# Loading all weight tiles of the eighth octet last in a fused linear-attention and spectral-mixing kernel

## The chip, the cores and the metric

The kernel runs on one core of a Trainium2 chip. The metric is the device time of one execution in microseconds (us); the span in a profile, from the first to the last instruction, is some 2 us shorter. A core has five engines that run side by side and wait for each other by semaphores: PE (matrix products, with its weight loads shown as PEld), DVE (elementwise work and reductions), ACT (activations, copies), POOL (elementwise work, and here the issuing of most transfers) and SP (issues transfers). Matrix products go to PSUM, eight banks in all; the other engines bring the results to SBUF. Transfers between the main memory and SBUF run on 16 DMA engines.

## What is computed

Two steps follow each other: a linear attention with a learned feature map, and a spectral mixing layer on its output.

```python
def phi(x):
    proj = np.einsum('bhsd,df->bhsf', x, w_phi)
    proj = proj - np.max(np.abs(proj), axis=-1, keepdims=True)
    return np.concatenate([np.exp(proj), np.exp(-proj)], axis=-1)
q_p, k_p = phi(q), phi(k)
kv = np.einsum('bhsf,bhsd->bhfd', k_p, v)
z = np.sum(k_p, axis=2)
num = np.einsum('bhsf,bhfd->bhsd', q_p, kv)
den = np.einsum('bhsf,bhf->bhs', q_p, z)[..., None] + 1e-06
x = num / den                      # as (batch, seq, heads * head_dim)

X = np.fft.rfft(x, axis=1)         # the first 64 modes are mixed, each by its own matrix
Yr = np.einsum('bmd,mde->bme', Xr, w_r) - np.einsum('bmd,mde->bme', Xi, w_i)
Yi = np.einsum('bmd,mde->bme', Xr, w_i) + np.einsum('bmd,mde->bme', Xi, w_r)
u = x + np.fft.irfft(Y, n=S, axis=1)
out = u + np.maximum(u @ w_ch, 0.0)
```

Batch 8, 8 heads, sequence 576, head size 64 (so 512 channels), 128 features, 64 modes. The matrices `w_r` and `w_i` are 64 x 512 x 512 each, in 4-byte floats, and are by far the most of what has to be read.

## The kernel before

**Tiles.** The 512 channels that go into the mixing are four groups `g` of 128 (two heads each), the 64 modes are eight octets `o` of eight. A weight tile holds, for one group and one octet, the eight matrices of either `w_r` or `w_i`: 64 tiles of 1024 KB each after the cast to 2-byte floats, keyed `(g, w)` with `w = 2 * o + i`. POOL issues their loads (`wload`, L341), most of them into a rotation of nine buffers `wt` (pool `pw`, L84); six tiles of the first group have homes in memory that is still free then, among them halves of `yacc`.

**Attention stage.** A unit is one group and two batches, 16 units in all. The loop from L504 runs over them as a pipeline: while one unit's q is exponentiated, the next one's k is, and so on. Each turn loads k, q and v of a later unit on POOL's queue and ends its part of `x` in `xs`; `freq` and `keep_x` transform a unit's rows to frequencies and put them into `XTb[g % 2]`, so that the rows of group 0 are overwritten by those of group 2, and those of 1 by those of 3. When the fourth unit of a group is done, the keys of the group's tiles are put into `mixq` (L521). `some(n)` (L489) takes keys from it in each turn (eight in the first turn, then three, once four): `mix` (L462) multiplies the frequency rows by the tile, in eight matmuls of 32 rows, and then `next_w(1)` (L360) issues the next load in the order of `wq`. The sum over groups is kept in `yacc` (512 4-byte floats per partition for each octet): group 0 is copied there by ACT, the others added by DVE.

**Order of the tiles** (L352 to L354): all 16 of group 0, all 16 of group 1, twelve of group 2, twelve of group 3 (octets 0 to 5), and then octet 6 of groups 2 and 3 (four tiles) and octet 7 of groups 2 and 3 (four tiles). The two groups of these last octets are summed in one PSUM tile; the sum of groups 0 and 1 is added from `yacc`.

**Loop at the end** (from L922). It takes the tiles that the attention stage has not used. After a mix it calls `next_w(1)`, but for three places (`left not in (19, 9, 8)`), as four of the nine buffers serve other tiles from now on (`yTa`, `zall`, `yall`, `yl`). When the last group of an octet is mixed, the octet's sum `yst` is transposed into `yTa` (octets 0 to 5) or, for octets 6 and 7, also multiplied by `w_ch` (`zst`) and sent by `put` (L818) to `yl`, with four small transfers: on POOL's queue for octet 6, on SP's for octet 7.

Between the mixes `fill(n)` (L813) takes entries from the list `todo`: 36 products (`product`: a chunk of `x` is transposed and multiplied by `w_ch`, the result is kept in `xw`; the first ones carry the tables of the inverse transform, on DVE, along), eight relays (`relay`: the octets so far, of one batch, are transposed into `yall` and multiplied by `w_ch` into `zall`), and 36 absorbs (`Absorb.all`: the modes of the octets so far are transformed back and added to the chunk in `xs` and in `xw`). For 14 of the absorbs (`aside`) the addition to `xw` is done by POOL. The count per mix is worked out from the number of entries left. All of `todo` is done before the last mix.

**After the last mix** comes a fixed order: the octet's sum, its transposes, `zst`, the transform of the last modes for all chunks (`Last`), the rectifier, the sum, and the stores on SP.

All engines' instructions stay in the order in which they are written (`keep_in_program_order`), so the order on each queue is the program's, and a waiting instruction holds up what stands behind it on its engine. POOL's queue holds tile loads, k, q and v loads, the aside additions and octet 6's `yl` transfers.

Of the kernel before, what the change touches and what calls it, by code (L numbers as in the profile page):

```python
# [44 lines left out]
def kernel(  # L45
# [303 lines left out]
        return wt  # L349

    wts = {}
    wq = [(g, mg) for g in range(2) for mg in range(2 * NO)]  # L352
    wq += [(g, mg) for g in (2, 3) for mg in range(12)]
    wq += [(g, 2 * o + i) for o in (6, 7) for g in (2, 3) for i in range(2)]  # L354
    order = list(wq)
    wq.remove((0, 5))
    wq.insert(1, (0, 5))
# [101 lines left out]
                                  op0=ALU.mult, op1=ALU.add)  # L459
    pys = {}  # L460

    def mix(g, w, wt, XT, bank):  # L462

        o, i = w // 2, w % 2
        late = g >= 2 and o >= 6
        first, last = i == 0 and not (late and g == 3), i == 1 and not (late and g == 2)
        if first:
            pys[o] = bank()
        py = pys[o]
        for r in range(2):  # L470
            for j in range(4):
                pe.matmul(
                    py[32 * j:32 * j + 32, :],
                    lhsT=XT[:, i, r, :, :, :, 4 * o + j].rearrange("p t x b -> p (t x b)"),
                    rhs=wt[:, j, r, :], start=(first and r == 0), stop=(last and r == 1),
                )
        if last and g == 0:
            act.copy(yacc[:, o, :], pys.pop(o))
        elif last and g < NG - 1:
            dve.tensor_tensor(  # L480
                out=yacc[:, o, :], in0=pys.pop(o), in1=yacc[:, o, :], op=ALU.add)
# [22 lines left out]
    for n in range(-2, len(units) + 1):  # L504
        P, Q, K, R = (unit(n + i) for i in (-1, 0, 1, 2))
        X = 0 if n < 4 or n == len(units) else 6 if n == 4 else 3
        if Q:
            Q.exp_q(0)
        if K:
            K.rows_k(0)  # L510
            K.exp_k(0)
        if Q:
            Q.weigh_v2()
            if unit(n + 2):
                unit(n + 2).load_v(sp if n + 2 == len(units) - 1 else pool)
        if P:
            P.freq()
            assert not any(key[0] == P.g - 2 for key in mixq)
            P.keep_x()
            if P.bp == NP - 1:  # L520
                mixq += [key for key in order if key[0] == P.g and (P.g < 2 or key[1] < 12)]  # L521
        if Q:
            Q.cols_q(1)
            Q.exp_q(1)
        some(1 if X else 0)
        if K:
            K.rows_k(1)
            K.exp_k(1)
        if Q:
            Q.kv()  # L530
        some(2 if n == 4 else 0)
        if K:
            K.rows_q(0)
            K.rows_k(2)
            K.rows_q(2)
            K.rows_q(1)
        if Q:
            Q.cols_q(2)
            Q.keep_kv()
            Q.exp_q(2)  # L540
        if K:
            K.exp_k(2)
            K.weigh_v()
        some(1 if X else 0)
        if R:
            R.turn_k(0)
        if K:
            K.shift_q()
        if R:
            R.turn_k(1)  # L550
        if Q:
            Q.num(0)
        if K:
            K.cols_q(0)
        if R and unit(n + 4):
            unit(n + 4).load_k()
        if Q:
            Q.num(6)
        if R:
            R.turn_q(0)  # L560
            R.turn_q(1)
            if unit(n + 4):
                unit(n + 4).load_q()
        if Q:
            Q.num(12)
        some(X - 2 + (n == 12) if X else 0)
        if n == -1:
            forward_table()
        if n < 3:
            next_w((2, 3, 2, 3, 2)[n + 2])  # L570
        elif n == 3:
            next_w(1)
        if n == 6:
            pool.dma_start(wchb, moe_w_ch.rearrange("(dc p) e -> p dc e", p=128))
    mixq += order[-8:]
    pm_cm.__exit__(None, None, None)
    pin_cm.__exit__(None, None, None)
    ps1_cm.__exit__(None, None, None)
# [200 lines left out]

    def relay(b):  # L780

        at = slice(0, 6 + (b < 2))
        n = 16 * at.stop
        cols = [yTa[:, dc, b, at].rearrange("p o k -> p (o k)") for dc in range(4)]
        py, pz = two_banks()
        py = py.bitcast(BF16)[:, 0:512]
        for dc in range(4):
            pe.transpose(py[:n, 128 * dc:128 * dc + 128], cols[dc], ident_b)
        for dc in range(4):
            pe.matmul(pz[:n], lhsT=cols[dc], rhs=wchb[:, dc, :],  # L790
                      start=(dc == 0), stop=(dc == 3))
        dve.tensor_copy(yall[:n, b], py[:n])
        act.copy(zall[:n, b], pz[:n])
# [8 lines left out]
        if chunks[i] in stored:  # L802
            ch[i].back_x()

    todo = [ch[0].turn] + [lambda i=i: product(i) for i in range(len(ch))]
    tail = [c.all for c in full]
    for at, b in ((24, 1), (22, 0), (17, 3), (14, 2), (7, 5), (5, 4)):
        tail.insert(at, lambda b=b: relay(b))
    tail = [lambda: relay(6), todo[-2], lambda: relay(7), todo[-1]] + tail
    A = len(tail)  # L810
    todo[-2:] = tail

    def fill(n):  # L813
        for _ in range(n):
            if todo:
                todo.pop(0)()

    def put(src, o, copies):  # L818
        for s in copies:
# [102 lines left out]
    while mixq:  # L922
        key = mixq.pop(0)
        g, o, i = key[0], key[1] // 2, key[1] % 2
        if key not in wts:
            next_w(1)
        if not mixq:
            assert not todo
            for c in seq[:2]:
                c.base(1)  # L930
            for c in (seq[0], seq[2]):
                c.base(0)
        mix(*key, wts.pop(key), XTb[g % 2], bank)
        left = len(mixq)
        if left not in (19, 9, 8):
            next_w(1)
        if left > 8:
            n = -(-max(len(todo) - A - 2, 0) // (left - 8))
        elif left == 8:
            n = 2  # L940
        else:
            n = math.ceil(len(todo) / max(left - 0.6, 0.4)) if left else 0
        if g == NG - 1 and i == 1:
            end = left == 0
            py = pys.pop(o)
            yst = pb.tile([128, DMODEL], BF16, name="yst")
            pt = [bank([128, 2, 128], BF16) for h in range(2)]
            yT = [pb.tile([128, 2, 128], BF16, name=f"yT{h}") if o > 5 else None
                  for h in range(2)]
            for h in range(2):  # L950
                dve.tensor_tensor(out=yst[:, H * h:H * h + H], in0=py[:, H * h:H * h + H],
                                  in1=yacc[:, o, H * h:H * h + H], op=ALU.add)
            if o > 5:
                put(yst, o, (0, 2))
            if not end:
                fill(min(n, 1))
            for h in range(2):
                for dc in range(2):
                    pe.transpose(pt[h][:, dc, :],
                                 yst[:, H * h + 128 * dc:H * h + 128 * dc + 128], ident_b)  # L960
                src = pt[h].rearrange("p c (k b) -> p c b k", b=B_)
                into = yTa[:, 2 * h:2 * h + 2, :, o] if o < 6 else None
                if h:
                    dve.tensor_copy(*((into, src) if o < 6 else (yT[h], pt[h])))
                else:
                    act.copy(*((into, src) if o < 6 else (yT[h], pt[h])))
            if o < 6:
                fill(n - 1)
                continue
            if o == 6:  # L970
                for h in range(2):
                    dve.tensor_copy(
                        yTa[:, 2 * h:2 * h + 2, 0:2, 6],
                        yT[h].rearrange("p c (k b) -> p c b k", b=B_)[:, :, 0:2])
            if end:
                seq[0].straight(0)
                seq[0].keep_p()
                seq[2].straight(0, (0,))
            else:
                fill(1)  # L980
            cut = (slice(0, 384), slice(384, DMODEL))
            pz = [bank([128, e.stop - e.start]) for e in cut]
            for e in range(2):
                for h in range(2):
                    for dc in range(2):
                        pe.matmul(
                            pz[e], lhsT=yT[h][:, dc, :], rhs=wchb[:, 2 * h + dc, cut[e]],
                            start=(h == dc == 0), stop=(h == dc == 1))
            zst = pb.tile([128, DMODEL], BF16, name="zst")
            act.copy(zst[:, cut[0]], pz[0])  # L990
            dve.tensor_copy(zst[:, cut[1]], pz[1])
            put(zst, o, (1, 3))
            fill(n - 2)
        else:
            fill(n)
    assert not todo
# [69 lines left out]
```

## Time and profile before

| | us |
|---|---|
| time, median of 3 runs (441.69 to 442.87) | 442.07 |
| time of the profiled execution | 440.27 |
| its span | 438.5 |
| PE busy | 333.7 (76%) |
| DVE busy | 300.9 (69%) |
| ACT busy | 282.3 (64%) |
| POOL busy | 111.9 (26%) |
| mean granted PE clock | 0.912 |
| data moved by DMA, mean rate | 97.71 MB, 223 GB/s |
| tile loads, median from issue to landing | 28.7 |

In a row of the timeline stand the start, the duration, the engine, the source line, the operation, out<-in, the shapes, how many instructions are merged, and in brackets how long the engine idled before and what ended that. All rows of the kernel proper show L38, the line of the helper that records every operation, so they are told apart by tile names: `wt,XT` is a mix, `wchb,xT` a product, `ident_b,xs` its transposes, `yall,CI` and `zall,CI` absorbs, `CF,xs` with 30 matmuls the transform to frequencies in attention, `yst` the octet's sum, `yl` the small transfers. Durations of matmuls overlap; the step from one start to the next is what one costs in a row. Tiles are numbered here 1 to 64 in the order of their mixing, so tile 64 is the last. In a transfer's row "us to landing" counts from the issue and includes the time spent in the queue.

### The profile page before, as it was taken

The page shows a single profiled execution, that of the slowest core. Times are in us where ns is not written, and L with a number is a line of the kernel's source. Part 1 is how long each engine was busy: PE and PEld are TensorE (multiplying, and loading weights), DVE is VectorE, ACT ScalarE, POOL GpSimd, SP SyncE. Part 2 cuts the span into 40 slices and gives each one's busy share as a digit, 9 for nine tenths or more (in the row PEclk, how much of TensorE's full clock was granted, in tenths as well). Part 3 has the DMA queues.
Part 4 walks back from the last instruction along what each step waited for, and adds up shares of the span by engine and source line. Part 5 has one row for each costly group of instructions (what it writes and reads, how often), then busy time and mean ns, then how long its engine had stood idle before and what let it go on. Part 6 is the DMA issues. An engine that isn't in the chain of part 4 may idle for free.

```text
span 438.5 us, 10103 instructions
## 1 busy us (share of the span) xinstructions
PE 333.7 (76%) x4208; PEld 203.0 (46%) x4252; DVE 300.9 (69%) x587; ACT 282.3 (64%) x483; POOL 111.9 (26%) x150
## 2 busy tenths in 40 slices
PE   2677658778777778787688687875898669998994
PEld 2345546646545555465455364533444335343421
DVE  5768598676784775887887858677734225786685
ACT  3688698688897585877876757526333225665682
POOL 6232122132221222222122121211022103651073
PEclk9989699699989596899998868969899899999997
DMA  9999999999999999999999999999999999990788
GB/s 217 209 212 210 238 213 236 238 212 249 227 211 238 227 229 228 237 216 233 233 216 238 233 239 212 212 212 212 212 212 212 212 212 212 212 204 27 239 339 333
DMA packets 49821, 97.71 MB, mean 223 GB/s; under 512 B 2288, under 2 KB 11632, under 8 KB 49776
## 3 DMA queue, kind: packets, MB, share of 16 engines
q0 software_dynamic: 45088, 85.27, 99.3%
q1 hardware_dynamic: 4528, 11.73, 7.4%
q8 instruction: 33, 0.54, 0.4%
q10 hardware_dynamic: 160, 0.07, 0.1%
q14 instruction: 12, 0.10, 0.1%
HBM read 163.64 MB, written 9.44 MB: 395 GB/s over the span
## 4 chain that ended last, share of the span: by engine, by line
DMA 39%; PE 26%; DVE 16%; ACT 11%; issue 5%; POOL 1%; POOLq 0%; ACTq 0%; DVEq 0%
DMA wt<-in_moe_w_r_dram 22%; DMA vn<-in_v_dram 12%; PE pt L38 9%; PE one L38 7%; PE pp L38 6%; DMA qb<-in_q_dram 5%; PE two L38 4%; ACT AB L38 4%; DVE m L38 3%; DVE mk L38 3%; ACT AQ L38 2%; DVE xs L38 2%; ACT xw L38 1%; DVE xw L38 1%; ACT XT L38 1%
## 5 line engine op out<-in xcount | busy, mean ns | idle before, releaser
L38 ACT ACTIVATE AB<-two 128x1024 bf16<-128x1024 f32 x64 | 62.0, 1025 | 14.6 <-DVE mk L38 11.3
L38 ACT ACTIVATE AQ<-two 128x1024 bf16<-128x1024 f32 x64 | 62.7, 1046 | 1.9 <-PE two L38 1.8
L38 ACT CAST xw<-pt 128x512 bf16<-128x512 f32 x45 | 26.4, 586 | 46.2 <-PE pt L38 46.2
L38 DVE TENSOR_REDUCE m<-two 128x8 f32<-128x1024 f32 x32 | 39.2, 1225 | 14.2 <-PE two L38 14.1
L38 PE MATMUL pt<-wchb,xT 128*128 128x512 bf16 x135 | 40.0, 410 | 7.6 <-DVE xT L38 5.8
L38 DVE TENSOR_TENSOR va<-vn,ee 128x1152 bf16<-128x1152 f32 x32 | 42.0, 1357 | 4.0 <-DMA vn<-in_v_dram 4.0
L38 DVE TENSOR_REDUCE mk<-two 128x8 f32<-128x1024 f32 x32 | 38.9, 1218 | 7.2 <-PE two L38 7.2
L38 POOL DMA_DIRECT2D wt<-in_moe_w_r_dram x30 | 22.3, 745 | 71.7 <-PE pt L38 30.9
L38 POOL DMA_DIRECT2D wt<-in_moe_w_i_dram x28 | 21.0, 749 | 76.0 <-PE one L38 38.6
L38 PEld LDWEIGHTS <-xs 128*128 128x128 bf16 x624 | 31.7, 103 | 13.6 <-issue 8.2
L38 PE MATMUL two<-w2blk,qT 128*128 128x256 bf16 x128 | 22.1, 301 | 20.0 <-ACT AB L38 9.0
L38 ACT COPY qT<-one 128x512 bf16<-128x512 bf16 (+1 forms) x32 | 19.3, 641 | 26.0 <-PE one L38 25.6
L38 PEld LDWEIGHTS <-qT 128*128 128x128 bf16 x144 | 14.7, 104 | 37.3 <-issue 34.0
L38 PE MATMUL two<-mT,minus 96*128 96x512 bf16 x64 | 27.1, 424 | 3.3 <-issue 1.5
L38 PEld LDWEIGHTS <-XT 128*32 128x32 bf16 x512 | 14.5, 149 | 31.5 <-issue 19.6
L38 PEld LDWEIGHTS <-AQ 128*128 128x128 bf16 x512 | 25.0, 109 | 7.6 <-issue 3.8
L38 PE MATMUL one<-wt,XT 128*32 128x512 bf16 x288 | 25.6, 442 | 3.9 <-DMA wt<-in_moe_w_i_dram 2.3
L38 PE MATMUL one<-kvz,AQ 128*128 128x65 bf16 x512 | 27.7, 210 | 1.0 <-ACT qT L38 0.8
L38 DVE TENSOR_TENSOR xs<-one,rd 128x384 bf16<-128x384 f32 x48 | 26.8, 557 | 1.6
L38 DVE COPY xT<-pt 128x512 bf16<-128x512 bf16 x36 | 16.8, 470 | 15.6 <-PE pt L38 15.6
L38 DVE RECIPROCAL rd<-one 128x6 f32<-128x6 f32 x48 | 9.4, 195 | 26.3 <-PE one L38 26.3
L38 PE MATMUL two<-w2blk,kT 128*128 128x256 bf16 x128 | 20.7, 289 | 8.7 <-ACT AB L38 8.7
(159 smaller groups left out, 731.2 us busy)
## 6 DMA issues: line engine op xcount, KB each, us to landing
wt<-in_moe_w_r_dram POOLq DMA_DIRECT2D x30, 1024.0 KB, 28.7
wt<-in_moe_w_i_dram POOLq DMA_DIRECT2D x28, 1024.0 KB, 28.7
out_dram<-of SPq DMA_DIRECT2D x16, 512.0 KB, 3.2
vn<-in_v_dram POOLq DMA_DIRECT2D x13, 576.0 KB, 25.0
kb<-in_k_dram POOLq DMA_DIRECT2D x16, 288.0 KB, 21.4
qb<-in_q_dram POOLq DMA_DIRECT2D x16, 288.0 KB, 20.7
xs<-in_moe_w_i_dram POOLq DMA_DIRECT2D x2, 1024.0 KB, 24.1
vn<-in_v_dram SPq DMA_DIRECT2D x3, 576.0 KB, 5.2
```

Source lines behind the costliest of these rows:

```text
L38: ins = f(*args, **kwargs)
```

## The change

The tiles that are mixed during attention (`during`) are now octets 0 to 6 of groups 0 and 1, and octets 0 to 5 of groups 2 and 3. Then follow the four tiles of octet 6 of groups 2 and 3, as before, and then all eight of octet 7, group by group. So 12 tiles and no longer 8 stand behind the attention stage's queue (`LATE`), and octet 6 is complete eight tiles before the end and no longer four. Octet 7 is summed over all four groups in one PSUM tile, and its row of `yacc` is not used for sums. As `XTb` is overwritten by later groups, POOL copies the rows of octet 7 of groups 0 and 1 into that row of `yacc` (`keep`, two copies each, after turns 6 and 8 of the attention loop), and `mix` reads them there.

The entries of `todo` carry an estimated length in us, `fill` takes entries until the length given is used up, and what was taken too much or too little is carried over. Every mix but the last two is given 3.4; the one before the last is given all that is left. The places without `next_w` are moved. After the last mix the sum need not be added to `yacc`, so it is two copies, one on DVE and one on ACT.

```diff
@@ -349,9 +349,11 @@
     wts = {}
-    wq = [(g, mg) for g in range(2) for mg in range(2 * NO)]
-    wq += [(g, mg) for g in (2, 3) for mg in range(12)]
-    wq += [(g, 2 * o + i) for o in (6, 7) for g in (2, 3) for i in range(2)]
+    during = (14, 14, 12, 12)
+    wq = [(g, mg) for g in range(NG) for mg in range(during[g])]
+    wq += [(g, 2 * o + i) for o in (6, 7) for g in range(NG) for i in range(2)
+           if 2 * o >= during[g]]
+    LATE = len(wq) - sum(during)
@@ -459,11 +461,22 @@
+    kept = yacc[:, NO - 1].bitcast(BF16).rearrange(
+        "p (g u r t x b m) -> p g u r t x b m", g=2, u=2, r=2, t=2, x=2, b=B_)
+
+    def keep(g):
+
+        for u in range(2):
+            pool.tensor_copy(
+                kept[:, g, u].rearrange("p r t x b m -> p (r t x b) m"),
+                XTb[g][:, u, ..., 4 * NO - 4:].rearrange("p r t x b m -> p (r t x b) m"))
+
     def mix(g, w, wt, XT, bank):
 
         o, i = w // 2, w % 2
-        late = g >= 2 and o >= 6
-        first, last = i == 0 and not (late and g == 3), i == 1 and not (late and g == 2)
+        together = range({6: 2, 7: 0}.get(o, g), NG) if 2 * o >= during[g] else (g,)
+        first, last = i == 0 and g == together[0], i == 1 and g == together[-1]
+        XT = kept[:, g] if o == 7 and g < 2 else XT[..., 4 * o:4 * o + 4]
@@ -471,7 +484,7 @@
-                    lhsT=XT[:, i, r, :, :, :, 4 * o + j].rearrange("p t x b -> p (t x b)"),
+                    lhsT=XT[:, i, r, :, :, :, j].rearrange("p t x b -> p (t x b)"),
@@ -518,7 +531,7 @@
-                mixq += [key for key in order if key[0] == P.g and (P.g < 2 or key[1] < 12)]
+                mixq += [key for key in order if key[0] == P.g and key[1] < during[P.g]]
@@ -570,9 +583,11 @@
+        if n in (6, 8):
+            keep(n // 2 - 3)
         if n == 6:
             pool.dma_start(wchb, moe_w_ch.rearrange("(dc p) e -> p dc e", p=128))
-    mixq += order[-8:]
+    mixq += order[-LATE:]
@@ -802,18 +818,21 @@
-    todo = [ch[0].turn] + [lambda i=i: product(i) for i in range(len(ch))]
-    tail = [c.all for c in full]
+    todo = [(0.5, ch[0].turn)]
+    todo += [(1.15 + 0.3 * (c in stored), lambda i=i: product(i)) for i, c in enumerate(chunks)]
+    tail = [(0.45 + 0.2 * (not c.aside) + 0.2 * (c.n == 8), c.all) for c in full]
     for at, b in ((24, 1), (22, 0), (17, 3), (14, 2), (7, 5), (5, 4)):
-        tail.insert(at, lambda b=b: relay(b))
-    tail = [lambda: relay(6), todo[-2], lambda: relay(7), todo[-1]] + tail
-    A = len(tail)
-    todo[-2:] = tail
+        tail.insert(at, (1.25, lambda b=b: relay(b)))
+    todo[-2:] = [(1.25, lambda: relay(6)), todo[-2], (1.25, lambda: relay(7)), todo[-1]] + tail
+    owed, turned = 0.0, 0
 
     def fill(n):
-        for _ in range(n):
-            if todo:
-                todo.pop(0)()
+        nonlocal owed
+        owed += n
+        while todo and owed > 0:
+            cost, f = todo.pop(0)
+            owed -= cost
+            f()
@@ -932,14 +951,9 @@
-        if left not in (19, 9, 8):
+        if left not in (LATE + 11, LATE + 1, LATE, LATE - 3):
             next_w(1)
-        if left > 8:
-            n = -(-max(len(todo) - A - 2, 0) // (left - 8))
-        elif left == 8:
-            n = 2
-        else:
-            n = math.ceil(len(todo) / max(left - 0.6, 0.4)) if left else 0
+        n = 3.4 if left > 1 else 99.0 if left else 0.0
@@ -948,24 +962,31 @@
             for h in range(2):
-                dve.tensor_tensor(out=yst[:, H * h:H * h + H], in0=py[:, H * h:H * h + H],
-                                  in1=yacc[:, o, H * h:H * h + H], op=ALU.add)
+                at = slice(H * h, H * h + H)
+                if not end:
+                    dve.tensor_tensor(out=yst[:, at], in0=py[:, at], in1=yacc[:, o, at],
+                                      op=ALU.add)
+                elif h:
+                    act.copy(yst[:, at], py[:, at])
+                else:
+                    dve.tensor_copy(yst[:, at], py[:, at])
             if o > 5:
                 put(yst, o, (0, 2))
             if not end:
-                fill(min(n, 1))
+                fill(0.8 if o != 5 else 0.0)
...
-                if h:
+                if h != end:
                     dve.tensor_copy(*((into, src) if o < 6 else (yT[h], pt[h])))
                 else:
                     act.copy(*((into, src) if o < 6 else (yT[h], pt[h])))
+            turned = o + 1
             if o < 6:
-                fill(n - 1)
+                fill(n - 1.1)
                 continue
...
             else:
-                fill(1)
+                fill(0.8)
...
             put(zst, o, (1, 3))
-            fill(n - 2)
+            fill(n - 2.4 if left else 0)
         else:
             fill(n)
```

An `assert` in `relay`, also new, states that the octets that a relay reads have been transposed.

## The prediction, made before the run

> **What bounds the kernel now.** First the slices of the span: PE busy, granted PE clock and busy DMA engines, 40 slices of 11 us.
>
> ```profile
> PE   2677658778777778787688687875898669998994
> PEclk9989699699989596899998868969899899999997
> DMA  9999999999999999999999999999999999990788
> ```
>
> The DMA engines are full until slice 36, at about 395 us; PE reaches nines only in slice 33. So transfers set the pace for long, and something else the end. The POOL timeline and the issues to landing date the last weight tile:
>
> ```profile
> 352.20 0.74 POOL L38 DMA_DIRECT2D wt<-in_moe_w_r_dram  x1 [4.18 <-PE pt L38]
> 370.32 0.79 POOL L38 DMA_DIRECT2D wt<-in_moe_w_i_dram  x1
> ...
> wt<-in_moe_w_i_dram POOLq DMA_DIRECT2D x1, 1024.0 KB, 25.5
> ```
>
> Tile 64 is issued at 370.3 and lands 25.5 us later, at 395.8. Tile 63 (issued 352.2, 38.6 to landing) lands at 390.8, tile 62 (347.3 + 38.6) at 385.9: one tile each 4.95 us, back to back. Now the PE timeline; each row of eight `wt,XT` matmuls is one mix:
>
> ```profile
> 336.37 0.66 PE L38 MATMUL pt<-wt,XT 128*32 128x512 bf16 x8 [1.05 <-DMA wt<-in_moe_w_i_dram]
> 341.38 0.66 PE L38 MATMUL pt<-wt,XT 128*32 128x512 bf16 x8 [1.46 <-DMA wt<-in_moe_w_r_dram]
> 346.31 0.66 PE L38 MATMUL pt<-wt,XT 128*32 128x512 bf16 x8 [1.99 <-DMA wt<-in_moe_w_i_dram]
> 351.23 0.66 PE L38 MATMUL pt<-wt,XT 128*32 128x512 bf16 x8 [0.24 <-DMA wt<-in_moe_w_r_dram]
> 356.18 0.66 PE L38 MATMUL pt<-wt,XT 128*32 128x512 bf16 x8 [2.00 <-DMA wt<-in_moe_w_i_dram]
> 361.20 0.66 PE L38 MATMUL pt<-wt,XT 128*32 128x512 bf16 x8 [1.47 <-DMA wt<-in_moe_w_r_dram]
> ...
> 399.54 0.66 PE L38 MATMUL pt<-wt,XT 128*32 128x512 bf16 x8
> 403.88 0.66 PE L38 MATMUL pt<-wt,XT 128*32 128x512 bf16 x8
> ```
>
> From 336 to 361 PE waits for tiles, 8.2 us in these six rows. After 361 it waits for none: the relays and absorbs pile up behind the mixes, and the last mix starts at 403.88, 8.05 us after its tile landed. The chain of waits says the same: a tile's transfer up to 361, then PE.
>
> ```profile
> 327.02 34.13 DMA wt<-in_moe_w_r_dram
> 361.15 0.04 issue
> 361.20 0.66 PE pt L38 x8
> ```
>
> After the last mix come 34.6 us (403.88 to 438.5) of PE-bound back transforms and stores, in which the change touches only the first two steps. So the question is: when does the last mix start?
>
> **The new landing of the last tile.** The same 64 tiles and inputs move, so if the queue never runs dry only the order can shift tile 64. It does: octet 6 is complete at tile 56 of 64 instead of 60, and its four `yl` transfers, which before were issued on POOL (382.4 to 387.0) behind all the tiles, now stand before tiles 62 to 64. Before, the last of them landed at 387.0 + 10.9 = 397.9, 2.1 us after tile 64; the first, at 382.4 + 14.2 = 396.6, 0.8 after it. Bounds: nothing, if full engines take small transfers in their stride, to four times 0.8, 3.2. I take the 2.1 seen, as the same four transfers on the same queue: tile 64 lands at 397.9. The diff doesn't show this cost.
>
> **Can PE be ready?** From the mix of tile 42 (286.74) to the last (403.88) lie 117.1 us; less the 8.2 of waits, 108.9 us of products, tables, relays, absorbs and mixes with their stalls. The loop now opens with tile 40, as two tiles of octet 7 leave the attention stage, so two mixes of 0.62 us (start to start of the next operation, 336.37 to 336.96) are added: 110.1. PE finished attention at 284.4 (rows of `CF,xs`, 283.27 + 1.15) and then idled 2.33 for tile 42; tiles 40 and 41 are there earlier. 284.4 + 110.1 = 394.5, 3.4 us before 397.9, counting no gain in attention (the two mixes taken out would save up to 1.1 each). The waits must not come back, though: per 4.95 us of transfer the new order gives PE at most three products (each 1.09: 341.98 to 343.07), a mix 0.62 and every second time the four `yst` transposes 0.2, about 4.1; in the absorb stretch at most 17 matmuls of 0.216 (376.88, 377.10) and a mix, 4.3. How good are such counts? From the mix at 361.20 to that at 368.21 they give two relays 2.2, two products 1.95 with their transposes, ten absorb matmuls 2.15 and a mix 0.62, 6.9 of 7.0 us; over all seven stretches to 403.88 they give 39.4 of 42.7, 8% of stalls. So 4.3 becomes 4.6, still under 4.95. PE therefore starts late (tables on DVE, as now), gains on the tiles, catches up near tile 57 to 62 and then waits for each. So the last mix starts at landing + 0.05: 397.95, a gain of 5.9.
>
> **Does the queue run dry?** The attention iteration after the first group's 14 tiles now has no mix, so POOL issues no tile where before it issued two (150.07 and 154.99), 9.9 us of transfer. At that spot `vn` (issued 148.67, 19.0 to landing) lands at 167.7; the next kb, qb and vn take about 1.4 each (kb 140.87 + 21.4 and qb 142.32 + 21.3 are 1.4 apart): busy to 172. The next tile goes out after the mix at 160.43, with 10.8 us still queued; after the mixes at 166.13 and 174.00, about 10 each time. The shortest issue to landing on this queue is 6.4 (kb, issued at 1.3). It stays fed: 0 us, up to 9.9 if that is wrong.
>
> **The smaller edits.** The four copies to `kept` stand on POOL ahead of wchb and of a vn. No row shows them; bounds 0 and 1.17 each (the 128x512 add on POOL), near the latter as a guess, 2.3 per pair. Between a tile issue about 174.8 and the vn at 179.5 POOL has 4 us, and before wchb 3.89 idle (waiting for a landing): 0 us; uncovered, 2.3 us of a 10 us reserve. Octet 7 loses its copy into yacc (ACT, 0.6) and its add (DVE, 0.68), and the last `yst` splits in two copies on two engines instead of two adds in 0.76 us on DVE: the second pair of transposes comes some 0.3 earlier, on the path: −0.3. Absorbs move with their POOL additions ahead of tile issues: the last four issues wait for up to four additions (1.16 each) and for the landing of tile 58, 59 or 60, with three tiles still in flight, 14.8 us: 0.
>
> **What idling costs PE.** Here a price appears that the diff doesn't tell. Windows of granted clock:
>
> ```profile
> 344.35:347.77 3.42, 1.46 (x15) 0.78 (x16) 0.74 (x3) 0.58 (x1) 0.48 (x1) 1.00 1.12 211
> 347.77:351.18 3.41, 3.00 (x13) 1.46 (x12) 1.19 (x4) 0.95 (x3) 0.26 (x1) 0.50 1.12 212
> 354.60:358.00 3.40, 1.82 (x19) 0.97 (x19) 1.09 (x3) 0.20 (x1) 0.00 (x0) 1.00 1.12 212
> ```
>
> (Columns: busy PE, PEld, DVE, ACT, POOL; clock; DMA.) A stretch of 3.4 us with PE busy 1.46 was followed by one at half clock; one with 1.82 was not. Before the last mix only five matmuls (1.1 us) remain besides the mix of tile 63 (0.62): of 5 us PE idles 3.2. That is under the level that lost the clock, so I expect half clock for one stretch at the start of the tail: bounds 0 and 1.7 (half of 3.4), taken 1.4, as part of it falls on waits.
>
> The Trainium skill (TensorE: Matmul & The Clock Gate, "The HAM clock gate") says that the clock falls after an idle window of about 3.4 us; on its word 3.2 us would cost nothing and the sum would be 1.4 lower. The row, where 43% of busy time was not enough, decides.
>
> **Sum.** 403.88 to 397.95: −5.9; `yst` −0.3; clock +1.4: −4.8 us. On the profiled execution, 440.27 (span 438.5), that is 435.5. The runs shown lie higher, median 442.07, so for a median I predict 442.07 − 4.8 = **437.3**.
>
> **Rivals.**
> - Nothing in the way (12%): the `yl` transfers cost tile 64 little and the clock holds: last mix about 395.9, −8.0 − 0.3: 433.8. For it: full engines may hide small transfers. Against: they landed one by one after the tile.
> - PE still late (15%): estimated lengths know nothing of the DVE tables (DVE busy 14.2 of 17 us from 293 to 310), PSUM or POOL. The margin is 3.4 us; with 7 us more of stalls the last mix starts at 401.5, without loss of clock: −2.4 − 0.3: 439.4.
> - The pacing does nothing (5%): the backlog of 8 us stays, the last mix near 404: 441.8, no change.
> - Slower (13%): the queue runs dry in attention, at the iteration without mixes, because vn, kb and qb wait for compute there and can't be issued earlier. All 9.9 us lost: tile 64 at 407.8, last mix 407.9, +4.0 − 0.3, and PE, idle before it, loses the 1.4 too: 447.2. It decides once the engines stand idle for more than 4.8 us in all. Against it: the 10 us of queue above.
>
> **How the numbers follow.** The forecast has 55%, its own range 435 to 439.5 (`yl` 0 to 3.2, clock 0 to 1.7, not both at their best). The range 433.5 to 441.5 adds the first three rivals nearly whole and leaves out the slow one. About 0.3%, 1.3 us, can be told from no change: faster means below 440.7. The forecast, the first rival and two thirds of the second give 0.77; the rest of the second and the third 0.10; slower 0.13.
>
> **What would show it.** Right: the last mix has a wait for a `wt` transfer before it, at 397 to 399; the `yl` issues stand before the last three tiles; DMA full throughout; one stretch of 0.50 clock near the last mix; 34 to 36 us from last mix to end. Wrong: last mix without a wait (PE late); a DMA slice under 9 between 150 and 200 us (dry); tile 64 landing before 396.5 (`yl` free).

## The result, and the profile after

| | before | changed |
|---|---|---|
| median, runs on one chip (us) | 441.88 (440.94 to 442.87, 4 runs) | 436.64 (435.59 to 437.91, 4 runs) |
| profiled execution (us) | 440.27 | 435.97 |
| its span | 438.5 | 434.2 |
| last mix, and from there to the end | 403.88, 34.60 | 399.55, 34.64 |
| mean granted PE clock | 0.912 | 0.905 |

The changed kernel takes 0.9882 of the time of before, 95% interval 0.9845 to 0.992. All of the gain in the span, 4.3 us, lies ahead of the last mix.

First the slices of the changed kernel: PE busy, granted PE clock, busy DMA engines.

```profile
PE   2577778688688578786787787957899999968994
PEclk9979697789998976989998988988899999997998
DMA  9999999999999999999999999999999999996788
```

The DMA engines stay at nine without a break up to slice 36, so the queue never ran dry. PE stays at nines from slice 29 to 34 (counted from 0), before only from 33 to 35. Its last transform of the attention stage ends at 281.02 in place of 284.42; that is within the scatter of this point from run to run (last section), so it is no sure effect of the change.

What the new order does show is where the relays begin. They read octets 0 to 5 (the last two of them octet 6 too), which are complete at tile 52 and no longer at tile 56. The first relay before, then tile 52's mix and the first relay of the changed kernel:

```profile
361.79 0.42 PE L38 MATMUL pp<-ident_b,yTa 128*96 128x128 bf16 x4
```

```profile
344.57 0.66 PE L38 MATMUL pt<-wt,XT 128*32 128x512 bf16 x8
...
347.30 0.39 PE L38 MATMUL pp<-ident_b,yTa 128*96 128x128 bf16 x4
```

The relays, and with them the absorbs, begin 14.5 us earlier.

The PE timeline of the changed kernel, the last four mixes (tiles 61 to 64):

```profile
381.89 0.66 PE L38 MATMUL pt<-wt,XT 128*32 128x512 bf16 x8
...
389.68 1.08 PE L38 MATMUL pt<-wt,XT 128*32 128x512 bf16 x8 [3.71 <-DMA wt<-in_moe_w_i_dram]
...
396.86 0.66 PE L38 MATMUL pt<-wt,XT 128*32 128x512 bf16 x8
...
399.55 0.66 PE L38 MATMUL pt<-wt,XT 128*32 128x512 bf16 x8 [0.63 <-DMA wt<-in_moe_w_i_dram]
```

Tile 62's mix waits 3.71 us for its transfer and the last one 0.63. No mix from 340 to 380 waits at all, as PE only catches up with the tiles at tile 61 (landed at 381.85). The chain of waits of the changed kernel agrees (start, length, what):

```profile
377.26 22.25 DMA wt<-in_moe_w_i_dram
399.55 0.68 PE pt L38 x8
```

The last tile's transfer, from issue to landing, now stands where PE's own work stood. Its landing is at 399.51. POOL's timeline shows what lies ahead of it in the queue:

```profile
361.53 0.78 POOL L38 DMA_DIRECT2D wt<-in_moe_w_r_dram  x1
362.31 1.09 POOL L38 DMA_DIRECT2D yl<-yst  x2
...
365.43 1.05 POOL L38 DMA_DIRECT2D yl<-zst  x2
...
367.59 0.79 POOL L38 DMA_DIRECT2D wt<-in_moe_w_i_dram  x1
...
377.26 0.78 POOL L38 DMA_DIRECT2D wt<-in_moe_w_i_dram  x1 [1.85 <-PE pp L38]
```

The four `yl` transfers are issued between tiles 61 and 62, and land between them, at 383.26 to 385.36. Tile 62 lands 7.79 us after tile 61 (389.64 against 381.85) where a tile alone takes 4.92: the `yl` transfers take 2.87. Their size would have given about that: four of 128 KB are half a tile of 1024 KB, so at the tiles' rate an estimated 2.5 us.

Last, the windows of granted clock of the changed kernel (columns as in the prediction):

```profile
385.50:388.92 3.42, 0.47 (x3) 0.13 (x1) 1.14 (x2) 1.43 (x3) 0.18 (x1) 1.00 1.12 213
388.92:392.33 3.41, 2.65 (x12) 0.78 (x12) 0.14 (x1) 0.00 (x0) 0.00 (x0) 0.50 1.12 212
392.33:395.75 3.42, 3.42 (x9) 1.06 (x7) 1.84 (x3) 1.73 (x3) 0.00 (x0) 0.50 0.93 174
395.75:399.16 3.41, 3.11 (x19) 1.06 (x19) 1.38 (x2) 1.17 (x2) 0.00 (x0) 1.00 0.49 91
```

The idle 3.71 us ahead of tile 62 cost two windows at half clock, ahead of the last mix and not behind it. They made tile 63's mix late (396.86, its tile landed at 394.56) and were taken up by the wait for tile 64: only 0.63 us of idle time was left there, and what follows the last mix ran at full clock to 429.88.

### The profile page after: what moved, and what is told of

The parts are those of the page before. It is cut to its first block, busy times and chain, and to the rows that moved or that the text cites. A ratio compares the mean times of both kernels' runs of the same rounds, so it can differ in the third digit from the quotient of the medians.

```text
span 434.2 us, 10105 instructions
## 1 busy us (share of the span) xinstructions
PE 336.4 (77%) x4208; PEld 202.1 (47%) x4252; DVE 298.6 (69%) x585; ACT 283.2 (65%) x483; POOL 114.4 (26%) x154
## 4 chain that ended last, share of the span: by engine, by line
PE 42%; DVE 22%; ACT 16%; DMA 12%; issue 6%; POOL 0%; POOLq 0%; ACTq 0%; DVEq 0%
PE pt L38 15%; PE one L38 15%; PE two L38 8%; ACT AB L38 7%; DMA wt<-in_moe_w_i_dram 5%; DVE mk L38 5%; DVE m L38 5%; DMA kb<-in_k_dram 5%; PE pp L38 4%; ACT AQ L38 3%; ACT XT L38 2%; DVE xs L38 2%; DMA qb<-in_q_dram 2%; DVE XT L38 2%; DVE yacc L38 1%
## 5 line engine op out<-in xcount | busy, mean ns | idle before, releaser
L38 ACT ACTIVATE AB<-two 128x1024 bf16<-128x1024 f32 x64 | 62.0, 1024 | 11.0 <-DVE mk L38 8.3
L38 PE MATMUL pt<-wchb,xT 128*128 128x512 bf16 x135 | 38.9, 400 | 9.3 <-DVE xT L38 7.3
L38 PE MATMUL two<-w2blk,qT 128*128 128x256 bf16 x128 | 23.5, 315 | 21.4 <-ACT AB L38 9.8
L38 PE MATMUL one<-wt,XT 128*32 128x512 bf16 x272 | 24.7, 452 | 1.7 <-DMA kb<-in_k_dram 1.7
L38 PEld LDWEIGHTS <-xT 128*128 128x128 bf16 x168 | 15.3, 103 | 21.9 <-DVE xT L38 8.0
```

The costliest lines, as they stand in the source:

```text
L38: ins = f(*args, **kwargs)
```

## The experiments

The runs were made on three chips, in groups of four kernels with runs of the kernel before beside them: medians of before 441.22, 441.29 and 441.10. Ratios below are to these. All are edits of the changed kernel.

**1. The `yl` transfers behind the last tile.** What does their place in the queue cost?

```diff
+        if o == 6:
+            owing.append((src, copies))
+            return
...
+    def put_owing():
+        while owing and not wq:
+            src, copies = owing.pop(0)
+            for s in copies:
+                pool.dma_start(yl[32 * s:32 * s + 16], src)
...
         if left not in (LATE + 11, LATE + 1, LATE, LATE - 3):
             next_w(1)
+        put_owing()
```

> Octet 6's four yl transfers are issued on POOL only after the last tile's load; nothing else differs from the changed kernel. Theory (the last mix waits for the last landing, and the yl transfers in front of tiles 62 to 64 cost about 2.9 us of it): tile 64 lands near 396.6 instead of 399.5, the last mix follows within 0.1 to 1 us, and the time falls by 1.5 to 2.9 us to 433.7 to 435.1; less than 2.9 only where PE, idle some 3 us before the last mix, gets half clock at the start of the tail. Rival (PE sets the last mix): tile 64 lands earlier but the last mix stays at 399 to 400, and the time at 436.6 plus or minus 1.

Measured: 434.72 us (434.32 to 435.69), ratio 0.9851 (0.9838 to 0.9864). Its PE timeline, tiles 63 and 64, and its windows:

```profile
391.93 0.66 PE L38 MATMUL pt<-wt,XT 128*32 128x512 bf16 x8 [0.28 <-DMA wt<-in_moe_w_r_dram]
397.32 0.66 PE L38 MATMUL pt<-wt,XT 128*32 128x512 bf16 x8 [3.55 <-DMA wt<-in_moe_w_i_dram]
```

```profile
395.50:398.92 3.42, 0.94 (x10) 0.32 (x10) 0.51 (x2) 0.37 (x1) 0.00 (x0) 1.00 0.37 92
398.92:402.33 3.41, 3.19 (x13) 1.75 (x15) 0.50 (x2) 1.44 (x3) 0.00 (x0) 0.50 0.33 77
```

Tile 64 lands at 397.28 and the last mix comes 2.23 us earlier; PE waits 3.55 us for it and was ready at 393.77. From the landing of tile 51 to that of tile 64 it takes 64.81 us here, 64.45 before and 67.36 in the changed kernel. But that idle time is now just ahead of the last mix, one window of the tail (the stretch from the last mix to the end) runs at half clock, and the tail takes 36.19 us in place of 34.64. So of 2.2 us gained 1.55 are given back in the profiled execution.

**2. The same transfers on SP's queue, at the old place.** Is it POOL's queue or the DMA engines that they hold up?

```diff
-            (pool if o == 6 else sp).dma_start(yl[r:r + 16], src)
+            sp.dma_start(yl[r:r + 16], src)
```

> Octet 6's yl transfers are issued by SP instead of POOL, at the same place of the program. If their price is the DMA engines' time, tile 64 still lands 2 to 3 us later than without them, near 399, and the time stays within 0.7 us of 436.6. If it is the place in POOL's queue (issue, descriptors, the wait for eight transfers in flight), tile 64 lands near 396.6 and the time is 434 to 435.

Measured: 437.59 us (436.68 to 438.91), ratio 0.9918 (0.9903 to 0.9932). The DMA issues of this kernel from 360 to 366 us (last columns: KB each, us from issue to landing):

```profile
yl<-yst SPq DMA_DIRECT2D x2, 128.0 KB, 8.5
yl<-zst SPq DMA_DIRECT2D x2, 128.0 KB, 9.3
```

From SP they land within 10 us, ahead of tiles that POOL issued before, and other tiles pay: tiles 58 and 59 take 5.81 and 5.97 us in place of 4.92. Tile 64 lands at 399.05, 66.56 us after tile 51. Of the price on POOL's queue 0.8 is saved; the larger part stays, and what the transfers use is time of full DMA engines. The time is 0.3 above the range given for this case; the clock accounts for that: the last mix waits 3.10 us, two windows of the tail run at half clock, and the tail takes 37.57.

**3. The order alone, and 4. the pacing alone.** The one keeps the old counts in `fill`, the other the old order, with estimated lengths; there a relay waits in `todo` until the octets it reads have been transposed, and the last sum is again added from `yacc`.

```diff
 # order alone
         owed += n
+        owed = n
...
-        n = 3.4 if left > 1 else 99.0 if left else 0.0
+        if left > LATE:
+            n = -(-max(len(todo) - A - 2, 0) // (left - LATE))
+        elif left == LATE:
+            n = 2
+        else:
+            n = math.ceil(len(todo) / max(left - 0.6, 0.4)) if left else 0
...
 # pacing alone
-    during = (14, 14, 12, 12)
+    during = (16, 16, 12, 12)
...
-        together = range({6: 2, 7: 0}.get(o, g), NG) if 2 * o >= during[g] else (g,)
+        together = range({6: 2, 7: 2}.get(o, g), NG) if 2 * o >= during[g] else (g,)
...
+            if getattr(todo[0][1], "needs", 0) > turned:
+                break
...
```

> The new order of tiles with the old pacing by counts (3 or 2 entries per mix until 12 tiles are left, then 4 or 5). Theory (the order gives the time in which absorbs can run, the pacing matters little): PE is ready for every late tile, the last mix waits for its landing at 399 to 400, time 436 to 437.5. Rival (the pacing by length is what removes the backlog): the last mix comes several us after the landing, time 439 to 442.

> The old order of tiles (8 late, octet 6 complete four tiles before the end, no kept rows) with the pacing by length; a relay waits in the list until its octets are turned. Counted by the old rows: products are done about tile 55, the first absorbs can start only after tile 56 (356), some 38 matmuls (8.2 us) are left after mix 63, so the last mix starts near 400 with tile 64 landed at 395.8: a gain of 3 to 4 us, time 438 to 439. Rival (order is all): last mix near 404 as before, time 441 to 442. Other rival (pacing is all): last mix at 396, time 434 to 435.

Measured: the order alone 437.25 us (436.27 to 439.18), ratio 0.9913 (0.9894 to 0.9932); the pacing alone 441.63 (441.13 to 442.48), ratio 1.0011 (1.0002 to 1.0019). The order brings the whole gain within what the runs can tell (0.9913 against 0.9882 for both edits, with intervals that overlap), and the expectation for the pacing alone was wrong. With the order alone the first relay starts at 345.72, and the last mix waits 1.30 us for its tile; two windows behind it then run at half clock, in a profiled execution that was the longest of the six. The PE timeline of the pacing alone (tiles 55, 56, 57 and 64) and its windows:

```profile
351.86 0.66 PE L38 MATMUL pt<-wt,XT 128*32 128x512 bf16 x8 [1.81 <-DMA wt<-in_moe_w_r_dram]
356.81 1.08 PE L38 MATMUL pt<-wt,XT 128*32 128x512 bf16 x8 [4.29 <-DMA wt<-in_moe_w_i_dram]
369.19 0.66 PE L38 MATMUL pt<-wt,XT 128*32 128x512 bf16 x8
...
405.62 0.66 PE L38 MATMUL pt<-wt,XT 128*32 128x512 bf16 x8
```

```profile
354.06:357.47 3.41, 0.66 (x8) 0.20 (x7) 0.00 (x0) 0.00 (x0) 0.00 (x0) 0.50 1.13 211
357.47:360.88 3.41, 2.74 (x15) 1.27 (x12) 1.18 (x3) 0.37 (x1) 0.00 (x0) 0.50 1.11 207
360.88:364.30 3.42, 3.20 (x15) 1.88 (x15) 0.85 (x2) 0.89 (x2) 0.00 (x0) 0.50 1.12 211
```

The products are done early and the relays may not start before octets 0 to 5 are complete, at tile 56, so PE waits 4.29 us for that tile, and from 354.06 on the clock is at half for 10.24 us. Thereafter the relays and absorbs pile up as they did before, and the last mix comes at 405.62, 8.79 us after its tile (396.83). Where the relays have to wait for tile 56, this pacing has nothing left to give PE in the gap.

**5. The clock kept.** To experiment 1 are added twelve matmuls into an unused bank ahead of the last mix; their results are not used.

```diff
             for c in (seq[0], seq[2]):
                 c.base(0)
+            idle = bank()
+            for _ in range(12):
+                pe.matmul(idle, lhsT=ident_b, rhs=wchb[:, 0, :], start=True, stop=True)
         mix(*key, wts.pop(key), XTb[g % 2], bank)
```

> The version with octet 6's yl transfers behind the last tile load (434.72 us, last mix 397.32, half clock for 3.41 us from 398.92, tail 36.19), plus 12 extra matmuls into an unused bank between the last base products and the last mix; their results are not used. Theory (the idle stretch before the last mix costs the clock at the start of the tail): the clock stays 1.0 through the tail, the tail goes back to about 34.6 and the time to 433.2 (432.5 to 433.9). Rival (the longer tail has another cause): the tail stays at 36.2 and the time at 434.7.

Measured: 433.02 us (432.76 to 433.74), ratio 0.9811 (0.979 to 0.9831). The PE timeline:

```profile
391.30 0.67 PE L38 MATMUL pt<-wt,XT 128*32 128x512 bf16 x8 [0.29 <-DMA wt<-in_moe_w_r_dram]
...
392.99 2.75 PE L38 MATMUL pt<-wchb,ident_b 128*128 128x512 bf16 x11
396.31 0.66 PE L38 MATMUL pt<-wt,XT 128*32 128x512 bf16 x8 [0.57 <-DMA wt<-in_moe_w_i_dram]
```

(One of the twelve is missing from the trace.) The idle time shrinks from 3.55 to 0.57, the clock stays at 1.00 to 427 us, and the tail takes 34.63 us, 1.56 less than in experiment 1. In the tail, the half clock was the whole price of the idle time. The last mix still stands 0.04 behind its landing.

**6. and 7. The changed kernel with its idle time filled.** One has 14 such matmuls ahead of tile 62's mix and 12 ahead of the last; the other has only the 14.

```diff
+        if len(mixq) == 2:
+            idle = bank()
+            for _ in range(14):
+                pe.matmul(idle, lhsT=ident_b, rhs=wchb[:, 0, :], start=True, stop=True)
         if not mixq:
```

> The changed kernel plus 14 extra matmuls ahead of the mix of tile 62 and 12 ahead of the last mix; their results are not used. Theory (the last tile's landing gates the end, and the half clock at 388.92 to 395.75 was swallowed by the wait for it): the mix of tile 63 comes at its landing, near 394.6 in place of 396.86, the last mix stays at the landing, near 399.5, the tail at 34.6, and the time is unchanged: 436.6, 435.9 to 437.3. Rival (the half clock ahead of the last mix cost time): the last mix comes 1 to 2 us earlier and the time is 434.6 to 435.6.

> The changed kernel plus the 14 extra matmuls ahead of the mix of tile 62 alone; their results are not used. Theory (the changed kernel escaped the clock price in its tail because the half clock fell ahead of the last mix and left little idle time there): the mix of tile 63 is on its landing, the idle time ahead of the last mix grows from 0.63 to about 3 us, the half clock falls into the tail, which grows by 1.5 to 3, and the time is 438.0 to 439.6 although TensorE was given work that kept its clock. Rival (no such trade): unchanged at 435.9 to 437.3.

Measured: both filled 436.31 us (436.1 to 436.83), ratio 0.9884 (0.9864 to 0.9904); only the first 437.32 (436.91 to 438.28), ratio 0.9911 (0.9891 to 0.993). Tiles 63 and 64 with both filled:

```profile
394.69 0.66 PE L38 MATMUL pt<-wt,XT 128*32 128x512 bf16 x8 [0.28 <-DMA wt<-in_moe_w_r_dram]
...
399.65 0.66 PE L38 MATMUL pt<-wt,XT 128*32 128x512 bf16 x8 [0.52 <-DMA wt<-in_moe_w_i_dram]
```

Both mixes are on their landings, no half clock falls from 300 to 429, and the time is the changed kernel's: the half clock ahead of the last mix, as its profiled execution had it, cost nothing. With the first alone, the clock is lost later; the windows of that kernel:

```profile
395.33:398.74 3.41, 1.21 (x8) 0.54 (x6) 0.00 (x0) 0.48 (x1) 0.00 (x0) 1.00 0.58 110
398.74:402.15 3.41, 1.92 (x13) 0.68 (x13) 0.71 (x2) 0.39 (x2) 0.00 (x0) 0.50 0.01 2
402.15:405.57 3.42, 3.42 (x13) 1.59 (x12) 0.29 (x1) 1.45 (x4) 0.00 (x0) 0.50 0.33 77
```

The last mix is at 399.69, 0.04 from the other's, but the tail takes 36.80 in place of 34.66. The theory's direction holds, as the ranges of the two kernels do not overlap, but its size does not: the medians lie only 1.0 apart, less than the 1.5 expected at least, and 437.32 is below the theory's 438.0 and at the upper end of the rival's range. The profiled execution (438.28) was the longest of its five, so its 36.80 is not the usual price.

**8. and 9. The keep copies doubled**, in the changed kernel and in that of experiment 5: eight copies on POOL in place of four.

```diff
-        for u in range(2):
+        for u in (0, 1, 0, 1):
```

> The changed kernel with its four keep copies on POOL made twice (8 copies, same data, same places). Theory (the copies lie on a queue that no transfer of that moment depends on): unchanged, 436.6 within 435.9 to 437.3. Rival (POOL's queue and its SBUF traffic delay the loads or VectorE there): the attention ends later and the time is 438.5 to 440.5, by as much as the copies' own 5.2 us at the most.

> The version that keeps the clock (433.02 us), with the four keep copies on POOL made twice, same data and places. The earlier doubling came out at 437.43 against 436.64 with the last tile landing no later (399.22) and half clock in the tail. Theory (the copies cost nothing, the 0.8 was the clock): 432.4 to 433.6, the last mix within 0.3 of 396.3 and the tail at 34.6. Rival (POOL's queue delays a load): the last tile lands 0.7 us or more later and the time is 433.8 to 434.5.

Measured: 437.43 us (435.89 to 438.9), ratio 0.9909 (0.9885 to 0.9933), in the first. That is just above the range expected. The last tile landed at 399.22, no later than without, but one window of the tail fell at half clock (36.18 us), so the first run alone didn't settle it. In the second: 433.58 (432.93 to 433.95), ratio 0.983 (0.9816 to 0.9843), the last mix at 396.49 and the tail 34.65. Four more copies, 0.7 to 1.9 us for a pair in the changed kernel's rows, delay no load that these runs can tell. The first run shows something else: its mix of tile 62 waits 2.45 us, the half clock behind that lasts one window and not two, PE then waits 1.87 us for tile 64, and the next window is at half clock. Where the idle time falls, and so whether the tail pays for it, differs between executions of almost the same kernel.

**10. The split of the last `yst` undone**, in the kernel of experiment 5.

```diff
-                elif h:
-                    act.copy(yst[:, at], py[:, at])
                 else:
                     dve.tensor_copy(yst[:, at], py[:, at])
```

> The version that keeps the clock (433.02 us), with both copies of the last yst on VectorE; the transposes' copies stay as they are. Theory (the split over two engines brings nothing, since ScalarE's copy starts only behind VectorE's): unchanged, 432.4 to 433.6, and from the last mix to the first transpose of the second pair the same 1.2 us within 0.1. Rival (the split is worth the 0.3 us predicted): about 433.3, and that stretch 0.3 longer; the profile tells them apart better than the times.

Measured: 433.12 us (432.86 to 433.22), ratio 0.9818 (0.9804 to 0.9831). The timelines of all engines behind the last mix, first of the changed kernel, then of this one:

```profile
400.26 0.42 DVE L38 CAST yst<-pt 128x256 bf16<-128x256 f32 x1 [2.59 <-PE pt L38]
400.72 0.37 ACT L38 CAST yst<-pt 128x256 bf16<-128x256 f32 x1 [2.44 <-DVE yst L38]
...
401.14 0.11 PEld L38 LDWEIGHTS <-yst 128*128 128x128 bf16 x2 [0.29 <-ACT yst L38]
```

```profile
397.54 0.76 DVE L38 CAST yst<-pt 128x256 bf16<-128x256 f32 x2 [5.61 <-PE pt L38]
...
398.35 0.11 PEld L38 LDWEIGHTS <-yst 128*128 128x128 bf16 x2 [0.22 <-DVE yst L38]
```

ACT's copy does not run beside DVE's but behind it: its row names DVE's `yst` as what it waited for, and it starts 0.04 us after that ends. The two copies share two tiles, the PSUM tile that both read and `yst`, of which each writes a half; no run shows which of them makes ACT wait. The second pair of transposes gets its weights 1.59 us after the last mix with the split (401.14 against 399.55; 1.59 in experiment 5 as well) and 1.52 without it (398.35 against 396.83). Before, with two adds on DVE, it was 1.53. The 1.2 us that the expectation names is the first pair's stretch, 1.19 in both kernels.

**11. Counts in place of lengths**, in the kernel of experiment 5, with the edit of experiment 3.

> The version that keeps the clock (433.02 us), with the old pacing by counts in place of estimated lengths, as in the run of the order alone. There the last mix (400.05) stood 1.30 us behind the end of PE's work, so PE was ready at about 398.7; here the last tile lands at 396.3. Theory (the pacing is worth something only once the tile lands early): PE is late, the last mix at 397.3 to 398.9 without a wait for its tile, and the time 434.0 to 435.6. Rival (pacing is worth nothing): 432.4 to 433.6, the last mix at its landing.

Measured: 435.05 us (434.42 to 435.38), ratio 0.986 (0.9847 to 0.9874). The number is the theory's, the reason only in part. The PE timeline, tiles 63 and 64:

```profile
391.81 0.66 PE L38 MATMUL pt<-wt,XT 128*32 128x512 bf16 x8
...
395.30 2.75 PE L38 MATMUL pt<-wchb,ident_b 128*128 128x512 bf16 x11
397.99 0.66 PE L38 MATMUL pt<-wt,XT 128*32 128x512 bf16 x8
```

The counts leave one absorb more for the time after tile 63: 3.49 us of PE (391.81 to 395.30) in place of 1.69 (391.30 to 392.99). With the added matmuls, 2.7 us, that is 6.18, where tile 64 lands 5.10 after tile 63, so the last mix is 1.08 late by this; it is 1.44 late in all, as tile 63's mix itself came 0.36 after its landing (391.45). In this execution attention ended at 286.05, the latest of all runs. Without the added matmuls the last mix would by these rows have been in time, as it was in experiment 3. So the run shows that the kernel of experiment 5 has no room there, not what lengths are worth by themselves; that stays open. In the changed kernel the medians with and without them, 436.64 and 437.25, lie 0.6 us apart, from different sets of runs that overlap.

**12. The kernel of experiment 5 again**, beside the last three.

> The version that keeps the clock once more, as the measure for the three runs beside it: 432.4 to 433.8 as before, the last mix within 0.3 of 396.3, no half clock from there to 427 and a tail of 34.6.

Measured: 433.78 us (433.18 to 434.49), ratio 0.9834 (0.982 to 0.9848). The last mix was at 397.27 without a wait, 1.08 after its tile, against the expectation; the tail took 34.66. In this execution PE ended attention at 283.93 (281.94 in the first), with 75.1 us at half clock ahead of 280 us against 58.0: here PE's own work, 113.3 us from there to the last mix without a wait for a tile, was the later of the two by 1 us. The version with late `yl` transfers and kept clock is the fastest tried, 433.0 to 433.8 us by its two medians.

## Why the prediction was right

The mechanism was that of the forecast: PE catches up with the tiles, the last mix waits for its landing, and the `yl` transfers make that landing later. The time, 436.64 against 437.3, came from a sum of which three terms were off.

**Landing, −5.9: measured −4.3.** The last mix stands 0.04 behind the landing of tile 64, as said, but at 399.55 and not 397.95. The `yl` transfers were mis-sized: 2.1 taken, 2.87 measured, inside the bounds 0 to 3.2; the same stretch, tile 61 to 62, was 2.3 to 2.7 longer than a tile in experiments 3, 6, 7 and 8 (the first kernel of it). Taking the time by which the last of them trailed tile 64 was too low; their size gives the nearer estimate, 2.5. The other 0.8 was not in the sum: the whole stream of tiles was later already at tile 51 (332.15 against 331.38). In the twelve experiments that landing lies between 331.35 and 332.63, and at 332.01 in experiment 4, which has the old order; so this is scatter and no sure cost of the change.

**PE ready at 394.5.** Right. Experiment 1 shows it best: PE was ready at 393.77, having ended attention at 282.30. That is 111.5 us, 110.7 without the waits for tiles 62 and 63 (0.45 and 0.28); taken were 110.1 (the rows given for a mix, 336.37 to 336.96, make 0.59 and not 0.62, which changes this by 0.06). Experiment 12 gives 110.6, its 113.3 less 2.75 of added matmuls. PE caught up with the tiles at tile 61, within the 57 to 62 given.

**Clock, +1.4: in the changed kernel's profiled execution 0.** The price is real, but its place was wrong. The sum let PE idle only ahead of the last mix; the longer idle time came at tile 62, as the `yl` transfers made just that tile late, and the half clock after it was hidden under the wait for tile 64. That it was hidden so well is in part luck: in experiment 8's first kernel, the same but for copies on POOL, the tail did pay. By the medians it was small all the same: experiment 6, where no half clock falls, took 436.31. Where the idle time did stand ahead of the last mix, the price was 1.55 us for one window (experiment 1, within the bounds) and 2.93 for two (37.57 less 34.64, experiment 2), above the bound of 1.7: the bound assumed a single window. The Trainium skill's idle window of about 3.4 us (TensorE: Matmul & The Clock Gate, "The HAM clock gate"), weighed in the prediction, would have put this price at nothing for the 3.2 us expected. The windows decide against that reading: 395.50 to 398.92 of experiment 1 had PE busy for 0.94 us and was followed by half clock. The idle time there was 3.55 us in one piece; in experiment 8's first kernel waits of 2.45 and 1.87 us, in windows with PE busy 1.54 and 1.23 us, were followed by half clock too.

**`yst`, −0.3: measured 0.** The split over two engines doesn't shorten anything, as ACT waits for DVE (experiment 10): 1.59 us to the second pair's weights against 1.53 before.

**The rest at 0.** Right: the queue stayed full, and the keep copies cost nothing that the runs can tell (experiments 8 and 9). The sum gives `vn` the 1.4 us of kb and qb, though it is twice their size (576 KB against 288); that only makes the queue longer.

Together the sum was −4.8, and the span fell by 4.3: the landing's +1.6 and the `yst`'s +0.3 against the clock's −1.4. The medians fell by 5.2, from 441.88 to 436.64, as both profiled executions lie below them, by unequal amounts. The near hit owes something to terms that cancel, and to that scatter. Of the signs named, the last mix came 0.55 after the stretch 397 to 399, and two windows at half clock stood where one was expected. Of the rivals, "nothing in the way" fell with the `yl` transfers; "PE still late" was avoided by some 3 us; "the pacing does nothing" holds of the pacing, but not of the change, whose gain is the order's (experiments 3 and 4): octets 0 to 5 are complete at tile 52 and no longer 56, and octet 6 eight tiles before the end, so the relays and the absorbs begin earlier (347.30 in place of 361.79).

## What to carry to other kernels

When units of work can only start once their inputs are complete, load what completes those inputs first: here that alone brought the gain, and pacing alone brought none. Where the last load gates the end and the DMA engines are full, small transfers ahead of it cost time: here some 2 to 2.9 us for four of 128 KB, on either queue. Issue what is needed only later behind the last load. PE may lose its clock when it then waits, and whether that costs anything depends on which wait comes next: a half clock was free under a later wait and cost 1.5 to 3 us on the way to the end. A copy split over two engines is worth nothing when the second half is made to wait for the first; the releaser in the row tells it at once.

## What was not expected of the hardware

- The clock went by how busy PE was in windows of 3.41 us, in both directions. Of the windows shown, those at full clock with PE busy 0.47, 0.94 and 1.21 us were followed by half clock. At half clock, windows with 0.66, 1.92, 2.65 and 2.74 were followed by half clock again, those with 3.19, 3.20 and 3.42 by full clock. Over all windows of the fourteen traces, none at full clock with less than 1.57 us kept it, and all above 1.8 did but for five (2.36 to 2.67) that began some 10 us before the end of a run; at half clock, none with less than 2.63 us brought it back, and all above 2.98 did. So PE at half clock gets it back only if it is hardly ever idle: in experiment 4 a wait of 0.53 us for DVE's `yst`, in the window with 2.74, helped to prolong it to 10.24 us.
- PE's end of attention, in code that is the same but for the POOL copies in all runs with the new order, lay between 279.3 and 286.05 us in the profiled executions, while the landing of tile 51 kept within 1.3 us. What PE has in hand ahead of the last tile varies by several us from run to run; in experiment 12 this made it the later of the two.
